# A dilated sliding attention with its feed-forward: ones written later and in blocks, one store on GpSimd, one q copy ahead of its reader

## The chip, the core and the metric

The kernel runs on one core of one Trainium2 chip. A core has four engines that compute, each with a queue of its own: TensorE (PE in the profile, its weight loads PEld), VectorE (DVE), ScalarE (ACT) and GpSimd (POOL). SyncE (SP) only issues transfers. Transfers run on 16 DMA engines and are issued from the queues of SP, ACT and POOL. The time of a run is device microseconds (us) from its begin to its end; lower is better. The change is judged by the median over runs.

## The reference

The inputs are q, k and v of shape 8 x 8 x 576 x 64 (batch, heads, tokens, width), and two weight matrices, w_in (512 x 2048) and w_out (2048 x 512). All are float32, and so is the output, of 4608 rows (8 x 576 tokens) by 512.

```python
rel = pos[:, None] - pos[None, :]
mask_plain = (rel >= 0) & (rel < window)                                    # window = 32
mask_dil = (rel >= 0) & (rel < window * dilation) & (rel % dilation == 0)   # dilation = 4
# heads 0..3 use mask_plain, heads 4..7 use mask_dil
scores = np.where(mask, scale * q @ k.T, -1e9)
attn = softmax(scores)
x = (attn @ v).transpose(0, 2, 1, 3).reshape(4608, 512)
h = np.maximum(x @ w_in, 0.0)
out = h * h @ w_out
```

## The kernel before, in words

Everything is computed in bfloat16 with float32 sums. The kernel is one long list of steps recorded in a fixed order; there is no loop on the chip. Each engine executes its own part of that list in order, and waits on semaphores where an operand or a buffer comes from another engine or from a transfer. Transfers have semaphores of their own, DMAHW0 to 7 for SP and ACT and DMASW0 to 7 for POOL, taken in turn; an issue first waits for the transfer that had its semaphore before it.

The feed-forward goes over tiles of tokens: four of 256 at first (two halves of each of two tiles), then seven of 512, 4608 tokens in all. Its work is cut into numbered groups. After each group some attention work for a later tile is recorded. Which work stands after which group is written out by hand in tables of strings: PROGRAM for batches 0 to 2 and the loads, STEPS for parts of batches 2 to 4 (an entry "57 2E20 ..." means: after group 57), STEADY for the tiles from token 1536 on, ALONE and LAST for the last two.

Attention works per batch on pairs of heads e = 0 to 3; e = 2 and 3 hold the dilated heads. Tokens are kept by their residue mod 4. For batches from 3 on, q and k are transposed by the DMA (line L334, issued by SP), and small vector copies then put border pieces where both halves of the partitions can read them: code Q (L571) copies the last or the first 16 tokens of each residue of q, code R (L596) those of k. `quadrants` (its matmuls are L724) computes the scores of one pair of heads and, in the same visit, the value products of other pairs, as 64 x 64 matmuls. In STEPS, "3V032/22,23" after group 59 is such a visit: scores of batch 3's pair 2, products of batch 2's pairs 2 and 3. "3Q0" is the q copy of batch 3 for the lower 64 partitions, whose target columns the last matmuls of that visit read. "W1" to "W4" are sums of weight blocks (L1010, `cross_w`), used from the tile at token 1536 on. L757 and L759 scale the value products into xT, the input of the feed-forward; L1067 is the first feed-forward product of the tiles up to 1535, L1230 the second one of the first four, L1138 and L1318 the products of later tiles.

The softmax's row sums are matmuls whose weights are `ones`, 128 columns at the end part of the constant tile mk: a 64 x 64 block of ones on the two diagonal places, zeros elsewhere. They are first used at L925. `bias` is another part of mk, made on VectorE from mask patterns that are loaded into mk at the start (L1411, on ACT's queue); L849 puts it into the scores of batch 0. `idle` is an area of zeros on which TensorE runs warm-up matmuls (L792) at the start.

The kernel begins with these constants, while POOL issues the loads of q, k, v and the weights one after the other (L267, L294, L1464). `load_qk` makes one issue for q and one for k.

Results leave through `store` (L968): 128 rows of the output tile osb are cut where the residue or the batch changes, and each piece is one issue. A batch has 576 tokens, 144 for each residue, so a piece can be short. Except for some stores of the last tile, all of them are issued by SP, as soon as VectorE (L1326) or ScalarE (L1347) has written the rows.

Of the kernel before, what the change touches and what calls it, by code (L numbers as in the profile page):

```python
# [75 lines left out]
FORKED = "BCD", "MNAB"  # L76
STEPS = (
# [33 lines left out]
def kernel(  # L111
# [9 lines left out]
    nc = tc.nc  # L121
    P = nc.NUM_PARTITIONS
    B, H, S, D = q.shape
# [43 lines left out]
    ones = mk[:, 256 + P : 256 + 2 * P]  # L167
# [613 lines left out]
    sides = [slice(64 * hl, 64 * hl + 64) for hl in range(2)]  # L781
# [172 lines left out]
    def store(osb, pos: int, c0: int = 0, c1: int = DM, engines=(nc.sync,)):  # L954

        x = turns = 0
        while x < P:
            b, y = divmod(pos + x, S)
            part = int(y >= RES * MN[0]) if b in PARTED else 0
            w = MN[part] if b in PARTED else M  # L960
            r, m = divmod(y - RES * MS[part], w)
            n, first = min(P - x, w - m), RES * (MS[part] + m) + r
            if b == B - 1:
                r, m = divmod(y, 16) if y < 64 else divmod(y - 64, 128)
                n, first = (16, RES * m + r) if y < 64 else (min(P - x, 128 - m), 64 + RES * m + r)
            row = b * S + first
            engine = engines[turns % len(engines)]
            engine.dma_start(out[row : row + RES * (n - 1) + 1 : RES, c0:c1], osb[x : x + n, c0:c1])  # L968
            x += n
            turns += 1  # L970
# [50 lines left out]
    def ffn_groups(tk0: int, nt: int):  # L1021
# [200 lines left out]
        def g2(m, part):  # L1222
            if part == 0:
                cur[m] = ps_f.tile([P, DM], f32, name="pf")
            x = m % 2 if per == 1 else m
            for f in range(4 * part, 4 * part + 4):
                n = 1 + ((tk0, m, part) in HALVED)
                for y in range(n):
                    cs = slice(y * DM // n, (y + 1) * DM // n)
                    nc.tensor.matmul(  # L1230
                        cur[m][:, cs],
                        h2[:, m // 2 if per == 1 else hh, HF * (f % 2) + f // 2, P * x : P * x + P],
                        w_out_sb[:, f, cs],
                        start=(f == 0 and y == 0), stop=(f == NF - 1), skip_group_check=True,
                    )
            if part == 3:
                slot = slots[0] = (slots[0] + 1) % (NT // P)
                nc.scalar.copy(osb[:, slot, :], cur[m][:, :])
                store(osb[:, slot, :], tk0 + (P * m + half) % nt if over else tk0 + P * m)
# [14 lines left out]
        def g2_small(code):  # L1254
# [8 lines left out]
            if code[0] == "P":  # L1263
                nm, a, b, fresh = {
                    "P1": ("y", b11, b_of[:, 0, 0], True), "P2": ("x", b12, b_of[:, 1, 0], True),
                    "P3": ("z", b12, b_of[:, 1, 1], False), "P4": ("y", b22, twin[1], False),
                    "P5": ("z", b21, t1, True), "P6": ("y", sm, t2, False), "P7": ("y", b11, twin[0], False),
                }[code[:2]]
                for k in range(*{"a": (0, HF // 2), "b": (HF // 2, HF), "": (0, HF)}[code[2:]]):
                    nc.tensor.matmul(  # L1270
                        place(nm), a[:, k, :], b[:, k, :], start=fresh and k == 0, stop=(k == HF - 1),
                        skip_group_check=True,
                    )
            elif code in "suz":
                to, nm = {"s": (outs[1][0], "y"), "u": (outs[0][1], "y"), "z": (outs[1][1], "z")}[code]
                nc.scalar.copy(to, place(nm))
            elif code in "ABCD":
                to, a, b, op = {"A": (b21, b21, b22, ALU.add), "B": (sm, b21, b11, ALU.subtract),
                                "C": (b11, b22, sm, ALU.subtract), "D": (b12, b12, sm, ALU.subtract)}[code]
                nc.vector.tensor_tensor(out=to, in0=a, in1=b, op=op)  # L1280
            elif code == "21":
                nc.scalar.copy(outs[1][0], place("y"))
                store(osb[:, cur["slots"][1], :], tk0 + P)
            else:
                to, nm = {"11": (outs[0][0], "x"), "12": (outs[0][1], "z"), "22": (outs[1][1], "y")}[code]
                nc.vector.tensor_tensor(out=to, in0=place(nm), in1=outs[1][0] if code == "11" else to, op=ALU.add)
                if code == "12":
                    store(osb[:, cur["slots"][0], :], tk0)
# [126 lines left out]
        nc.vector.memset(t[64:128, :, :, 0:64], 0.0)  # L1415

    nc.vector.memset(idle[:, :], 0.0)
    nc.vector.memset(ones[:, :], 0.0)
    for rows in sides:
        nc.vector.memset(ones[rows, rows], 1.0)  # L1420
    plain = osb[:, 0, :].rearrange("p (e i d) -> p e i d", e=2, d=D)
    for e in range(2):
        for hl, rows in enumerate(sides):
# [3 lines left out]
    for es, bs in ((slice(0, NE // 2), slice(0, NB)), (slice(NE // 2, NE), slice(8, NB))):  # L1427
        for hl in range(2):
            to = vbd[0][64 * hl : 64 * hl + 64, es, bs, 64 - 64 * hl : 128 - 64 * hl]
            none = idle[64 * hl : 64 * hl + 64, 0:64].unsqueeze(1).unsqueeze(1).broadcast_to(list(to.shape))  # L1430
            nc.scalar.copy(to, none)
    nc.vector.tensor_scalar(out=bias, in0=mk[:, 0:256], scalar1=-1.0, scalar2=30000.0, op0=ALU.add, op1=ALU.mult)
    far_end = osb[:, 1, 0:128].rearrange("p (e d) -> p e d", e=2)
    for hl, rows in enumerate(sides):
        nc.sync.dma_start(far_end[rows, :, :], v[0, H // 2 + hl : H : 2, 512:S, :].rearrange("h p d -> p h d"))
# [157 lines left out]
```

## Time and profile before

| what | value |
|---|---|
| median of 3 runs | 281.95 us (281.3 to 281.96) |
| the profiled execution | 281.38 us |
| its span, first to last instruction | 279.6 us |
| granted TensorE clock, mean | 0.997 |
| TensorE busy | 271.4 us, 97% of the span |
| VectorE, ScalarE, GpSimd busy | 227.6, 206.2 and 128.5 us |
| moved by DMA | 36.93 MB |

A row of the timeline or of the chain begins with its start and its duration in us, then the engine, the line of the kernel, the operation with what it writes and reads, the number of instructions merged into the row, and in brackets the idle time of the engine before it and what ended that. SPq, ACTq and POOLq are the queues that issue transfers. Rows of grouped lines end with busy us and the mean ns of one. A row on DMA issues ends with the time from issue to landing in us. A tile's number is left out in names: qk holds the transposed q and k, qb and kb what was loaded of them, pt the weights of the softmax, rec the reciprocals of its sums, h2T the hidden layer; pf, pa, po and pd are PSUM tiles.

### The profile page before, as it was taken

To read this page: it belongs to the slowest core of one execution; us is meant where nothing else is said; L and a number is where in the kernel's file an instruction comes from. 1 tells how busy PE (TensorE), PEld (TensorE's weight loads), DVE (VectorE), ACT (ScalarE), POOL (GpSimd) and SP (SyncE) were. 2 spreads that over 40 slices of the span, in tenths; PEclk is the share of its full clock that TensorE was granted. 3 is DMA by queue.
4 is the path that set the end of the run, shared out by engine and by line. 5 is a ranking of instruction groups with operands and counts; after the bars stand their busy time and mean duration, and the time that the engine had idled before them with its cause. 6 is when DMAs were issued, how large, how long until landed. Compare 5 with 4: busy or idle time off the path is not lost.

```text
span 279.6 us, 9042 instructions
## 1 busy us (share of the span) xinstructions
PE 271.4 (97%) x3681; PEld 234.4 (84%) x3687; DVE 227.6 (81%) x475; ACT 206.2 (74%) x457; POOL 128.5 (46%) x209
## 2 busy tenths in 40 slices
PE   7899999999999999999999999999999999999994
PEld 3679988997954578899889988988898899989983
DVE  0886998787789987879977997899699778965973
ACT  6888768887986878898689778977886667327620
POOL 8769973484872687764784359750000000000000
PEclk9999999999999999999999999999999999999998
DMA  8999999999999999999989996930310040013003
GB/s 127 198 193 213 207 152 220 196 144 212 187 193 225 153 172 198 183 198 173 166 83 221 193 149 94 181 26 4 98 55 2 2 152 0 2 38 113 4 24 129
DMA packets 83786, 36.93 MB, mean 132 GB/s; under 512 B 52736, under 2 KB 78464, under 8 KB 83744
## 3 DMA queue, kind: packets, MB, share of 16 engines
q0 software_dynamic: 49040, 18.53, 58.1%
q1 hardware_dynamic: 33728, 17.33, 30.9%
q10 hardware_dynamic: 976, 0.49, 0.7%
q8 instruction: 29, 0.48, 0.7%
q14 instruction: 13, 0.11, 0.1%
HBM read 37.31 MB, written 9.44 MB: 167 GB/s over the span
## 4 chain that ended last, share of the span: by engine, by line
PE 93%; DMA 2%; issue 1%; ACT 1%; DVE 1%; POOL 0%; POOLq 0%
PE pf L1318 31%; PE pf L1067 15%; PE pf L1138 10%; PE pf L1230 7%; PE pa L1138 7%; PE pd L1138 5%; PE po L1138 4%; PE pf L1270 2%; DMA kb<-in_k_dram 2%; PE pa L724 2%; PE pf L724 1%; PE po L724 1%; PE pa L354 1%; PE pd L724 1%; PE pa L819 1%
## 5 line engine op out<-in xcount | busy, mean ns | idle before, releaser
L1318 PEld LDWEIGHTS <-h2T 128*128 128x128 bf16 x680 | 64.4, 98 | 9.0 <-DVE h2T L1349 0.2
L1318 PE MATMUL pf<-w_out_sb,h2T 128*128 128x256 bf16 x448 | 53.4, 273 | 0.0
L552 POOL DMA_DIRECT2D vbd<-in_v_dram x80 | 42.9, 545 | 19.8 <-DMA vbd<-in_v_dram 5.8
L1067 PE MATMUL pf<-xT,w_in 128*128 128x256 bf16 (+1 forms) x319 | 44.6, 294 | 0.7 <-issue 0.7
L968 POOL DMA_DIRECT2D out_dram<-osb x1 | 0.6, 610 | 88.3 <-DVE osb L1326 88.3
L1067 PEld LDWEIGHTS <-w_in 128*128 128x128 bf16 x320 | 34.3, 114 | 7.9 <-issue 1.4
L1138 PEld LDWEIGHTS <-w_in 128*128 128x128 bf16 x288 | 31.6, 114 | 0.9 <-issue 0.3
L1080 ACT ACTIVATE h2T<-pf 128x512 bf16<-128x512 f32 x48 | 26.6, 603 | 4.8 <-PE pf L1067 4.5
L1347 ACT COPY osb<-pf 128x512 f32<-128x512 f32 x22 | 12.8, 583 | 19.3 <-PE pf L1318 16.4
L1200 DVE TENSOR_TENSOR h2T<-h2T 128x1024 bf16<-128x1024 bf16 x40 | 26.1, 683 | 0.1
L1230 PE MATMUL pf<-w_out_sb,h2T 128*128 128x256 bf16 (+1 forms) x139 | 22.5, 305 | 0.5 <-issue 0.3
L1326 DVE TENSOR_TENSOR osb<-pf,osb 128x512 f32<-128x512 f32 (+1 forms) x22 | 14.8, 674 | 7.8 <-ACT rec L741 5.1
L1138 PEld LDWEIGHTS <-qb 128*128 128x128 bf16 x192 | 21.0, 113 | 0.0
L1146 ACT ACTIVATE h2T<-pf 128x512 bf16<-128x512 f32 x28 | 16.8, 619 | 1.7 <-PE pf L1138 1.7
L1230 PEld LDWEIGHTS <-h2T 128*128 128x128 bf16 x144 | 13.2, 98 | 5.1
L544 POOL DMA_DIRECT2D vbd<-in_v_dram x20 | 12.1, 620 | 10.4 <-DMA qb<-in_q_dram 4.6
L1138 PE MATMUL pf<-xT,w_in 128*128 128x256 bf16 x112 | 16.8, 273 | 0.0
L1150 DVE CUSTOM_DVE_ANT_0 h2T<-pf,kb 128x512 bf16<-128x512 f32 x16 | 10.6, 685 | 7.3 <-PE pf L1138 5.2
L288 POOL DMA_DIRECT2D vbd<-in_v_dram x16 | 10.9, 689 | 10.9 <-DMA kb<-in_k_dram 4.9
L538 POOL DMA_DIRECT2D vd<-in_v_dram x20 | 12.2, 624 | 5.5 <-DMA kb<-in_k_dram 3.4
L750 ACT ACTIVATE rec<-rec 128x576 f32<-128x576 f32 x22 | 14.2, 688 | 0.3
L1085 DVE TENSOR_TENSOR h2T<-h2T 128x1024 bf16<-128x1024 bf16 (+1 forms) x20 | 11.4, 583 | 3.3 <-ACT h2T L1080 2.9
(267 smaller groups left out, 697.3 us busy)
## 6 DMA issues: line engine op xcount, KB each, us to landing
out_dram<-osb SPq DMA_DIRECT2D x20, 128.0 KB, 5.3
qb<-in_q_dram POOLq DMA_DIRECT2D x7, 320.0 KB, 8.6
kb<-in_k_dram POOLq DMA_DIRECT2D x7, 320.0 KB, 11.1
vd<-in_v_dram POOLq DMA_DIRECT2D x32, 64.0 KB, 6.7
w_in<-in_moe_w_in_dram POOLq DMA_DIRECT2D x4, 512.0 KB, 7.5
w_out_sb<-in_moe_w_out_dram POOLq DMA_DIRECT2D x4, 512.0 KB, 11.8
qb<-in_q_dram POOLq DMA_DIRECT2D x7, 256.0 KB, 7.5
kb<-in_k_dram POOLq DMA_DIRECT2D x7, 256.0 KB, 9.8
```

Of the source, the lines that this page charges most:

```text
L552: nc.gpsimd.dma_start(v_rows[b % 2][p0 + 16 * r : p0 + 16 * r + 16, e, :, :], v[b, 2 * e + hl, :, :].rearrange("(i m r) d -> r m i d", r=R ...
L724: nc.tensor.matmul(out, lhs, rhs, start=begin, stop=True, skip_group_check=True)
L750: nc.scalar.activation(rec[:, :], rec[:, :], ACT.Exp, scale=-1.0)
L1067: nc.tensor.matmul(to, w_in_sb[piece][:, kt, c0 : c0 + 509 : 4], rhs, start=(kt == kts[0] and x == 0), stop=(kt == kts[-1] and x == per - ...
L1080: nc.scalar.activation(hv, acc[u][:, :].rearrange("p (x n) -> p x n", x=2), ACT.Relu)
L1138: nc.tensor.matmul(home(nm)[:, g, :], wk[:, c0 + g : c0 + g + 127 * step + 1 : step], rhs[:, kt, :], start=fresh and kt == 0 and g == 0, s ...
L1146: nc.scalar.activation(to, home(nm), ACT.Relu)
L1200: nc.vector.tensor_tensor(out=part, in0=part, in1=part, op=ALU.mult)
L1230: nc.tensor.matmul(cur[m][:, cs], h2[:, m // 2 if per == 1 else hh, HF * (f % 2) + f // 2, P * x : P * x + P], w_out_sb[:, f, cs], start=( ...
L1318: nc.tensor.matmul(bank(nm, m, cs.start)[:, m, cs], a[:, k, P * m : P * m + P], w[:, cs], start=fresh and k == ks[0] and (m == 0 or nm == ...
L1326: nc.vector.tensor_tensor(out=to[:, at, cs], in0=src[:, at, cs], in1=other[:, at, cs], op=ALU.add)
L1347: nc.scalar.copy(bank("x") if code == "s" and forked_out else to, bank(nm))
```

## The change

It has three parts.

1. The zeroing of `ones` moves behind the bias. The two blocks of ones, 64 x 64 each, are then written by sixteen memsets of 64 x 8 in place of two.
2. In `store`, a piece of exactly 16 rows of batch 6 (B - 2) is issued by GpSimd in place of SP. There is one such piece in the program.
3. In STEPS, the copy 3Q0 stands after group 57 in place of group 60.

```diff
-    "3R01 | 58 W1 | 59 W2 3V032/22,23 2L2 W4 | 60 3Q0 W3 2X2 2L3 | 61 2X3 | 62 3Y0 | 63 3E20 | 64 3Y1 3K0 | 65 "
+    "3R01 3Q0 | 58 W1 | 59 W2 3V032/22,23 2L2 W4 | 60 W3 2X2 2L3 | 61 2X3 | 62 3Y0 | 63 3E20 | 64 3Y1 3K0 | 65 "
...
-            engine = engines[turns % len(engines)]
+            engine = nc.gpsimd if b == B - 2 and n == 16 else engines[turns % len(engines)]
...
     nc.vector.memset(idle[:, :], 0.0)
-    nc.vector.memset(ones[:, :], 0.0)
-    for rows in sides:
-        nc.vector.memset(ones[rows, rows], 1.0)
...
     nc.vector.tensor_scalar(out=bias, in0=mk[:, 0:256], scalar1=-1.0, scalar2=30000.0, op0=ALU.add, op1=ALU.mult)
+    nc.vector.memset(ones[:, :], 0.0)
+    for hl, rows in enumerate(sides):
+        for x in range(64 * hl, 64 * hl + 64, 8):
+            nc.vector.memset(ones[rows, x : x + 8], 1.0)
```

On VectorE, at the begin of the program, with the semaphores that each row waits for (DMAHW2 is the load of the mask patterns, Activation is ScalarE):

```order
 L1417 MEMSET qk 128x128
-L1418 MEMSET mk 128x64
-L1420 MEMSET mk 64x64 [waits DVE_49]
-L1420 MEMSET mk 64x64
-L1432 TENSOR_SCALAR mk<-mk 128x256 [waits DMAHW2_49]
+L1429 TENSOR_SCALAR mk<-mk 128x256 [waits DMAHW2_49]
+L1430 MEMSET mk 128x64
+L1433 MEMSET mk 64x8 [waits DVE_49]
+L1433 MEMSET mk 64x8 x15
 L834 COPY qk<-pa 128x256 [waits Activation_49] x2
```

The bias (TENSOR_SCALAR) now follows the zeroing of `idle` directly, and all memsets of `ones` stand between it and the first copy of transposed data.

On VectorE, around the visit after group 59 (L571 is 3Q0, the L596 copies are 3R00 and 3R01, the L1010 rows W1, W2, W4 and W3; DMAHW2 is here the transposed q):

```order
 L596 COPY qk<-qk 64x128 [waits DMAHW1_49]
 L596 COPY qk<-qk 64x128
+L571 COPY qk<-qk 64x4x2x16 [waits DMAHW2_49]
 L1010 TENSOR_TENSOR qb_96<-w_in_88 128x1024 [waits DMASW2_49,DMASW0_49,Pool_49]
 L1010 TENSOR_TENSOR qb_96<-qb_96,w_in_87 128x1024 [waits DMASW0_49,DVE_49]
 L1010 TENSOR_TENSOR qb_96<-w_in_87,qb_96 128x1024 [waits DMASW4_49,DVE_49]
-L571 COPY qk<-qk 64x4x2x16 [waits DMAHW2_49,PE_49]
 L1010 TENSOR_TENSOR qb_96<-w_in_87,w_in_88 128x1024 [waits DMASW1_49]
-L757 TENSOR_TENSOR xT<-po,rec 128x4x128 [waits Activation_49]
+L757 TENSOR_TENSOR xT<-po,rec 128x4x128 [waits PE_49,Activation_49]
```

The copy moved ahead of three sums. Its wait for TensorE is gone (before, it waited for the matmuls of the visit that read its target), and L757 now carries the wait for TensorE. On TensorE, in that visit, the 18th of the 20 score matmuls and its neighbours:

```order
 L724 MATMUL pa<-qk 64x80
 L724 LDWEIGHTS qk [waits DVE_49]
-L724 MATMUL pa<-qk 64x64
+L724 MATMUL pa<-qk 64x64 [waits DVE_49]
 L724 LDWEIGHTS qk
 L724 MATMUL pa<-qk 64x64
```

The order of TensorE's instructions is the same; the first matmul that reads the copied columns now waits for VectorE. In the queue of POOL, at its end, one row is new:

```order
 L552 DMA vbd_104<-in_v_dram 16x9x64 [waits DMASW4_49]
 L552 DMA vbd_104<-in_v_dram 16x9x64 [waits DMASW5_49]
-L968 DMA out_dram<-osb 128x256 [waits DMASW6_49,DVE_49]
-L1588 UNCONDITIONAL_BRANCH
-L1588 ISA [waits barrier_Pool_Activation_PE_DVE_SP_gather]
+L968 DMA out_dram<-osb 16x512 [waits DMASW6_49,DVE_49,Activation_49]
+L968 DMA out_dram<-osb 128x256 [waits DMASW7_49,DVE_49]
+L1589 UNCONDITIONAL_BRANCH
+L1589 ISA [waits barrier_Pool_Activation_PE_DVE_SP_gather]
```

The store of 16 rows stands between POOL's last load and its one store of the last tile.

## The prediction

> **What bounds the kernel now.** I read the page's busy times first, then its chain, then busy time by stretches of the span, then the timeline at the three places that the change touches.
>
> ```profile
> PE 271.4 (97%) x3681; PEld 234.4 (84%) x3687; DVE 227.6 (81%) x475; ACT 206.2 (74%) x457; POOL 128.5 (46%) x209
> PE 93%; DMA 2%; issue 1%; ACT 1%; DVE 1%; POOL 0%; POOLq 0%
> 2.00:12.00 10.00, 8.74 (x173) 5.30 (x173) 3.97 (x11) 7.23 (x19) 9.59 (x16) 1.00 1.24 185
> 12.00:30.00 18.00, 17.34 (x267) 15.94 (x261) 13.65 (x31) 15.18 (x32) 14.50 (x16) 1.00 1.28 204
> 80.00:90.00 10.00, 9.83 (x125) 5.12 (x125) 9.31 (x22) 6.62 (x15) 3.41 (x7) 1.00 1.40 210
> 120.00:249.00 129.00, 129.00 (x1806) 117.37 (x1805) 112.86 (x201) 96.47 (x207) 43.55 (x78) 1.00 0.63 95
> 249.00:256.00 7.00, 6.99 (x65) 6.67 (x63) 2.40 (x4) 4.44 (x9) 0.00 (x0) 1.00 0.50 150
> ```
>
> The last five rows give, after the stretch and its length, the busy time of PE, PEld, DVE, ACT and POOL. TensorE is the chain (93%), and from 120 to 249 us it has no hole at all. An edit elsewhere can win only what TensorE idles in the edit's own stretch: 1.26 us at 2 to 12, 0.66 at 12 to 30, 0.17 at 80 to 90, 0.01 at 249 to 256. It can lose more, by making TensorE wait.
>
> **Part 1, the ones.** Before, VectorE writes them in three memsets and then idles until the constants land; the bias follows, and then it idles again:
>
> ```profile
> 0.98 0.11 DVE L1418 MEMSET mk<- 128x64 uint32 x1
> 1.16 0.28 DVE L1420 MEMSET mk<- 64x64 bf16 x2
> 2.71 0.23 DVE L1432 TENSOR_SCALAR mk<-mk 128x256 bf16<-128x256 bf16 x1 [1.27 <-DMA mk<-mask_patterns]
> L1420 DVE MEMSET mk<- 64x64 bf16 x2 | 0.2, 112 | 0.1
> 6.62 0.38 ACT qk L833
> 7.03 0.76 DVE L834 COPY qk<-pa 128x256 bf16<-128x256 bf16 x2 [4.09 <-ACT qk L833]
> 10.05 0.21 PEld L925 LDWEIGHTS <-mk 128*128 128x128 bf16 x4
> ```
>
> The bias starts when its data lands (2.71 us) whether or not memsets stand ahead, so nothing is won there. Behind it now stand 17 memsets. A memset of a 64x8 block is not in the trace; the nearest row is 64x64 at 112 ns, and two of those took 0.28 us from start to end, so they start 0.28 - 0.112 = 0.168 us apart. From below: 17 x 0.112 = 1.9 us, done at 2.94 + 1.9 = 4.8. From above: 16 x 0.168 + 0.112, and some 0.06 for the wait on the zeroing (0.98 + 0.112 to 1.16): 2.9 us, done at 5.8. VectorE's next copy cannot start before ScalarE's copy ends (6.62 + 0.38 = 7.00), and TensorE's first weights from the ones load at 10.05. I take the upper end, since a row of several memsets shows that spacing: 1.2 us of cover stay. Without the cover (over 0.24 us per memset) each further 0.1 us would go straight into the copy at 7.03, which the chain passes through. Cost on the path: 0.
>
> The other neighbour is POOL, which issues the first loads through exactly this time:
>
> ```profile
> 1.27 0.74 POOL L267 DMA_DIRECT2D qb<-in_q_dram  x1 [0.82 <-POOLq L1577]
> 3.21 0.64 POOL L267 DMA_DIRECT2D kb<-in_k_dram  x1
> 6.29 0.84 POOL L1464 DMA_DIRECT2D w_in<-in_moe_w_in_dram  x1
> 7.78 0.64 POOL L267 DMA_DIRECT2D kb<-in_k_dram  x1
> 7.83 0.48 DVE L1414 MEMSET vbd<- 64x512 uint32 x1
> w_in<-in_moe_w_in_dram POOLq DMA_DIRECT2D x1, 512.0 KB, 6.7
> 13.57 0.45 PEld L1067 LDWEIGHTS <-w_in 128*128 128x128 bf16 x4 [0.22 <-issue]
> ```
>
> An issue of the same kind took 0.64 us beside an idle VectorE (3.21) and 0.64 us beside a VectorE memset (7.78 against 7.83), so I take no interference. The bounds: at most POOL slips by the whole memset time at 112 ns, 1.9 us; of that the first weights' load hides 13.57 - (6.29 + 6.7) = 0.58 us, leaving 1.3 us on TensorE. On the gain side, the first issue (0.74) ran beside the old memsets and would take 0.64 without them: 0.1 us off the first load, on which the chain starts. Taken: 0; ends -0.1 and +1.3.
>
> The Trainium skill, "SBUF — State Buffer", section "Who interferes with whom", says that a VectorE instruction with at most one SBUF input and outside the two-port modes does not contend with GpSimd; a memset has none, so by that rule the sum here is 0. The same page warns in its "DVE blocks DMA" box that VectorE copies from SBUF to SBUF can keep GpSimd from writing descriptors; if that held for memsets too, the sum would be the +1.3 us. The 7.78 row agrees with the first.
>
> **Part 2, the store.** One issue of 16 rows leaves SP's queue and joins POOL's.
>
> ```profile
> 248.00 1.51 DVE L1326 TENSOR_TENSOR osb<-pf,osb 128x512 f32<-128x512 f32 x2 [0.34 <-PE pf L1318]
> 249.54 0.33 SPq L968 DMA_DIRECT2D out_dram<-osb  x1
> 253.87 0.88 SPq L968 DMA_DIRECT2D out_dram<-osb  x2
> 266.67 0.59 ACT L1347 COPY osb<-pf 128x512 f32<-128x512 f32 x1 [1.15 <-PE pf L1318]
> 273.91 0.61 POOL L968 DMA_DIRECT2D out_dram<-osb  x1 [88.35 <-DVE osb L1326]
> 275.51 0.29 DVE osb L1326
> ```
>
> It is the first of the eleven that SP issues from 249.54 to 254.75 us, so the ten behind it go 0.33 us sooner. On POOL it costs what POOL's one store costs, 0.61 us, and it waits for the same VectorE sum (249.51). POOL has nothing else between 185 and 273.91 us, so nothing is queued behind it but the last quarter, 24 us later. The next writer of its output slot is the last tile's copy at 266.67 or later, some 14 us behind, so a store slower by any factor seen here is still hidden. SP's completion semaphores shift by one place; each stands for a store eight issues back, landed long before. The chain ends in the last VectorE sum (275.51 + 0.29 = 275.80) and its store, which keep their engines. Sum: 0; from the rows not below -0.01 (TensorE's whole idle there), not above +0.05.
>
> **Part 3, the q copy.** Now it stands ahead of three of the four weight sums of L1010, and the matmul that reads its columns waits for it.
>
> ```profile
> 73.70 1.48 SPq L334 DMA_TRANSPOSE qk<-qb  x1
> qk<-qb SPq DMA_TRANSPOSE x1, 6.4
> 81.56 0.52 DVE L596 COPY qk<-qk 64x128 bf16<-64x128 bf16 x2
> 82.10 0.69 DVE L1010 TENSOR_TENSOR qb<-w_in 128x1024 bf16<-128x1024 bf16 x1
> 83.55 0.69 DVE L1010 TENSOR_TENSOR qb<-w_in,qb 128x1024 bf16<-128x1024 bf16 x1
> 84.28 0.19 DVE L571 COPY qk<-qk 64x128 bf16<-64x128 bf16 x1
> 84.50 0.69 DVE L1010 TENSOR_TENSOR qb<-w_in,w_in 128x1024 bf16<-128x1024 bf16 x1
> 85.11 0.68 DVE L757 TENSOR_TENSOR xT<-po,rec 128x512 bf16<-128x512 f32 x1
> 86.44 0.68 DVE L757 TENSOR_TENSOR xT<-pf,rec 128x512 bf16<-128x512 f32 x1
> 82.55 0.20 PE pa L724 x20
> 87.17 0.01 issue
> 117.48 0.59 PE pd L1138 x4
> 87.18 2.92 PEld L1067 LDWEIGHTS <-w_in 128*128 128x128 bf16 x14 [0.27 <-issue]
> ```
>
> The copy's one remaining wait is for the transposed q, which landed at 73.70 + 6.4 = 80.1 us, 2 us ahead. So it follows the two L596 copies, from 82.1 to 82.3. Its reader is the 18th of the 20 matmuls that run from 82.55 to 82.75 on the chain, so at 82.7: 0.4 us to spare. The three sums behind it start about 0.2 us later; they feed the products of L1138, which first run at 117.48 us. The fourth sum needs no result of the third, so the gap where the copy stood closes: 84.50 - 84.24 = 0.26 us come back against 0.19 paid, and the L757 sums start where they did or up to 0.1 us sooner. TensorE's hole at 87.17, just behind the second L757 (ends 87.12), is 0.01 us on the chain and 0.27 us in weight loads. Taken: 0. From below -0.17 us (all of TensorE's idle at 80 to 90); from above +0.2 us (the copy's length, if every VectorE step slips by it into 87.17).
>
> **Sum.** 0 + 0 + 0. The profiled run took 281.38 us for a span of 279.6, 0.57 below the median of 281.95; the runs reach from 281.3 to 281.96, so the profile is of a run at their lower end. On the median I forecast 281.9 us. Differences under 0.3% (0.85 us) cannot be told from none here, since three runs of one kernel already spread by 0.66 us.
>
> **Rivals.** First, slower: the memsets hold up POOL's issues. For it speaks only that both run at 3 to 6 us; against it the equal issues of 0.64 us. Its full price is +1.3 us, 283.2 us, and it passes 0.3% once POOL slips by 0.85 + 0.58 = 1.43 us, that is 84 ns for each of 17 memsets. Chance 0.10. Second, slower by little: VectorE's line slips by the copy, or TensorE waits for it; +0.2 us, 282.1 us, for it the meeting at 87.12 and 87.17, against it the gap that closes. Chance 0.12, within 0.3% by itself. Third, faster: the first load goes 0.1 us sooner, and TensorE's 0.17 us of idle at 80 to 90 go: 281.6 us, or some 281.1 where the median also falls among the lower runs (281.3). For it the 0.74 beside the 0.64; against it that TensorE's idle at 2 to 30 has other causes. Chance 0.18, of which 0.10 pass 0.3% if something unseen adds to it. My forecast, no effect, has 0.55; 0.05 stay for a slowing that none of these names.
>
> So slower by over 0.3% gets 0.10 + 0.05 = 0.15, faster 0.10, the rest 0.75. The range runs from 281.0 (the third rival at the lowest run) to 282.9 (most of the first rival on the median), leaving 2 in 10 outside.
>
> **What would show it.** Right: the memsets end before 6 us, the copy of L834 still starts near 7.0; POOL's third to sixth issues still take 0.63 to 0.69 us and TensorE's first w_in weights load near 13.6; L571 runs near 82.1 and the 82.55 group has no hole; SP's ten stores end near 254.4; the chain still ends in the sums of 275 us. Wrong: an issue of POOL at 3 to 6 us over 0.75 us, VectorE still in memsets at 7 us, a TensorE wait on L571, or a new wait of VectorE or ScalarE for the POOL store at 266 to 273 us.

## The result: faster by 0.4%, and most of it not where the change was costed

The changed kernel takes 280.41 us, the median of 6 runs (279.94 to 280.76). The kernel before, timed beside it, takes 281.47 us (6 runs, 281.3 to 281.96). The ratio is 0.9958, with a 95% interval of 0.9948 to 0.9968. The forecast was 281.9 us and no effect. Of the 1.49 us between it and the measurement, 0.43 lie in the kernel before: the forecast stood on a median of 281.95 us of three runs, and six give 281.47. The change itself is the other 1.06. The profiled execution after took 280.44 us with a span of 278.7 us; before, the span was 279.6 us.

The page of the changed kernel, busy times and chain:

```profile
PE 271.4 (97%) x3687; PEld 234.2 (84%) x3687; DVE 228.3 (82%) x489; ACT 206.3 (74%) x457; POOL 129.0 (46%) x210
PE 94%; DMA 2%; ACT 1%; issue 1%; DVE 1%; POOL 0%; POOLq 0%
```

TensorE still is the chain and as busy as before. VectorE has 489 instructions in place of 475: the 14 more memsets. At the two places where the prediction had costed work, the timeline of the changed kernel shows this (VectorE, then POOL, at 2.5 to 8 us; VectorE at 81 to 87 us):

```profile
2.69 0.23 DVE L1429 TENSOR_SCALAR mk<-mk 128x256 bf16<-128x256 bf16 x1 [1.68 <-DMA mk<-mask_patterns]
3.05 0.39 DVE L1433 MEMSET mk<- 64x8 bf16 x16
7.00 0.76 DVE L834 COPY qk<-pa 128x256 bf16<-128x256 bf16 x2 [3.56 <-ACT qk L833]
3.22 0.65 POOL L267 DMA_DIRECT2D kb<-in_k_dram  x1
...
81.39 0.49 DVE L596 COPY qk<-qk 64x128 bf16<-64x128 bf16 x2
81.78 0.19 DVE L571 COPY qk<-qk 64x128 bf16<-64x128 bf16 x1
84.07 0.68 DVE L1010 TENSOR_TENSOR qb<-w_in,w_in 128x1024 bf16<-128x1024 bf16 x1
84.67 0.68 DVE L757 TENSOR_TENSOR xT<-po,rec 128x512 bf16<-128x512 f32 x1
86.00 0.68 DVE L757 TENSOR_TENSOR xT<-pf,rec 128x512 bf16<-128x512 f32 x1
```

The sixteen memsets are done at 3.44 us, POOL's issue beside them takes 0.65 us, and the copy of L834 starts at 7.00. The q copy stands ahead of the sums, and the gap that it left has closed: the first L757 sum starts 0.44 us sooner.

The end of the kernel differs. First VectorE's last sum, then the last store (issued by ScalarE's queue; the last number is us from issue to landing), then SyncE's waits at the end of the program (total, times, longest), before:

```profile
275.51 0.29 DVE L1326 TENSOR_TENSOR osb<-pd,osb 128x128 f32<-128x128 f32 x1
out_dram<-osb ACTq DMA_DIRECT2D x1, 128.0 KB, 2.4
SPq L1588 <- DMA out_dram<-osb: 2.8, 2, 2.0
L1588 SPq DRAIN  x3: 7/7/13, 278.8 to 279.1; - x3
```

and the same views after:

```profile
275.48 0.29 DVE L1326 TENSOR_TENSOR osb<-pd,osb 128x128 f32<-128x128 f32 x1 [0.15 <-PE pd L1318]
out_dram<-osb ACTq DMA_DIRECT2D x1, 128.0 KB, 1.9
SPq L1589 <- DMA out_dram<-osb: 1.9, 4, 0.7
L1589 SPq DRAIN  x3: 7/7/13, 277.8 to 278.1; - x3
```

The last sum ends at 275.80 us before and 275.77 after: up to there these two executions come out equal (what lies behind that is told with the copy below). From its end to the end of the span it takes 3.80 us before and 2.90 after. I call this stretch the tail. Its two parts, in the records of the trace:

- The last store lands 2.36 us after its issue before, and 1.89 after.
- From that landing to the end of the span it takes 1.36 us before, and 0.92 after.

Together 0.03 + 0.47 + 0.44 us, which is the whole difference of the spans. The busy time of the engines shows nothing of it, since no engine computes there.

**The first part is an instruction fetch.** DMA by queue kind, and the busy tenths of the DMA engines in 40 slices, first from 276 to 277 us and then from 277 to 278, before:

```profile
q10 hardware_dynamic: 183, 0.17, 50.1%
q1 hardware_dynamic: 153, 0.13, 40.8%
q14 instruction: 1, 0.01, 1.9%
...
DMA  9996682200010010101011010110101000000000
```

The same stretch, 277 to 278 us, after (from 276 to 277 us its list holds only q10 and q1):

```profile
DMA  7956542100000000000000000000000000000000
```

q14 carries instructions in packets of 8192 bytes, and not VectorE's alone. It has thirteen of them in the span, before and after. Eight lie within 0.9 us of each other in the two executions. The other five move with the 14 instructions that VectorE has more: from 37.25, 80.21, 137.78, 196.59 and 276.48 us to 26.89, 76.55, 131.33, 190.12 and 263.49. I take these five for VectorE's. Before, the last one starts at 276.48 us, 0.97 us behind the start of the last sum, and holds one of the 16 DMA engines for 309 ns. The last store is spread over all 16. Fifteen have finished their share 1.89 us after the issue; the one with the packet takes until 2.36. That is the row of single ones from 277.2 to 277.8 us. After, it lies at 263.49 us and the slices are empty from 277.2 us.

**The second part is the order in which SyncE waits.** At the end of the program SyncE waits for the transfers' semaphores in nine waits, one after the other and always in the same order; for one that is already done the next wait starts 0.062 us later. Before, the last store had the second semaphore of that list, and seven waits followed once it had landed: 7 x 0.062 = 0.43 us. In the view of waits SyncE waits twice, 2.0 us of it at once. After, one store fewer from SyncE shifts the semaphores by one place, and the last store has the last one on the list: four short waits while the stores land one by one, and nothing behind the last.

### The profile page after: what moved, and what is told of

Same layout as the page of the kernel before. It is cut to its first block, busy times and chain, and to the rows that moved or that the text cites. A ratio compares the mean times of both kernels' runs of the same rounds, so it can differ in the third digit from the quotient of the medians.

```text
span 278.7 us, 9063 instructions
## 1 busy us (share of the span) xinstructions
PE 271.4 (97%) x3687; PEld 234.2 (84%) x3687; DVE 228.3 (82%) x489; ACT 206.3 (74%) x457; POOL 129.0 (46%) x210
## 4 chain that ended last, share of the span: by engine, by line
PE 94%; DMA 2%; ACT 1%; issue 1%; DVE 1%; POOL 0%; POOLq 0%
PE pf L1318 31%; PE pf L1067 15%; PE pf L1138 11%; PE pf L1230 8%; PE pa L1138 7%; PE pd L1138 5%; PE po L1138 4%; PE pf L1270 2%; PE pa L724 2%; DMA kb<-in_k_dram 2%; PE pf L724 1%; PE po L724 1%; PE pa L354 1%; PE pd L724 1%; PE pa L819 1%
## 5 line engine op out<-in xcount | busy, mean ns | idle before, releaser
L1230 PE MATMUL pf<-w_out_sb,h2T 128*128 128x256 bf16 (+1 forms) x144 | 23.3, 308 | 0.0
L267 POOL DMA_DIRECT2D qb<-in_q_dram x18 | 13.2, 735 | 3.4 <-DMA vbd<-in_v_dram 1.8
```

The source lines that it names most:

```text
L267: nc.gpsimd.dma_start(t[0:n, part, hs, :], src[b, hs, t0 : t0 + RES * n, :].rearrange("h (p r) d -> p h (r d)", r=RES))
L1230: nc.tensor.matmul(cur[m][:, cs], h2[:, m // 2 if per == 1 else hh, HF * (f % 2) + f // 2, P * x : P * x + P], w_out_sb[:, f, cs], start=( ...
```

## The experiments

The working theory was these two parts, with the first owed to the number of VectorE's instructions (part 1 of the change adds 14) and the second to part 2. The rival was that one of the parts wins its time in the body, where the prediction had looked for it. In the table, "added" is the number of VectorE instructions added ahead of 30 us. "Gap" is the time between VectorE's wait ahead of a sum of L981 (at 35 us; used further below) and that sum. "Fetch" is the start of the last q14 packet against the start of the last sum. "Landed" is from the issue of the last store to its landing, "behind" from there to the end of the span, and "tail" is the stretch defined above. All these come from the one profiled execution. "Median" is less the median of the kernel before in the same job. All in us. The ratios in the text, with their 95% intervals, are not taken from these medians and can differ from them: the 0.9977 of e8 is 0.65 us, its median 1.00.

| kernel | added | gap | fetch | landed | behind | tail | median |
|---|---|---|---|---|---|---|---|
| before | 0 | 0.47 | +0.97 | 2.36 | 1.36 | 3.80 | |
| after | 14 | 0.07 | -11.99 | 1.89 | 0.92 | 2.90 | -1.06 |
| e1 ones only | 14 | 0.07 | -12.16 | 1.97 | 1.35 | 3.41 | -0.81 |
| e2 store only | 0 | 0.48 | +1.00 | 2.39 | 0.92 | 3.40 | -0.46 |
| e3 copy only | 0 | 0.48 | +0.98 | 2.37 | 1.35 | 3.81 | -0.08 |
| e4 two memsets | 0 | 0.47 | +1.00 | 2.38 | 0.92 | 3.39 | -0.59 |
| e5 memsets ahead | 14 | 0.07 | -12.15 | 1.89 | 0.92 | 2.90 | -1.27 |
| e6 four memsets | 2 | 0.07 | -1.49 | 1.90 | 0.92 | 2.92 | -1.21 |
| e7 eight memsets | 6 | 0.06 | -5.85 | 1.89 | 0.92 | 2.90 | -1.25 |
| e8 four stores | 14 | 0.06 | -11.88 | 1.93 | 1.11 | 3.13 | -1.00 |
| e9 four, old place | 2 | 0.06 | -1.30 | 1.90 | 1.35 | 3.34 | -0.87 |
| e10 one column each | 128 | 0.43 | +1.02 | 2.41 | 0.92 | 3.42 | -0.63 |
| e11 without the copy | 14 | 0.07 | -12.14 | 1.89 | 0.92 | 2.90 | -1.00 |
| e12 changed, again | 14 | 0.07 | -12.16 | 1.90 | 0.92 | 2.91 | -1.34 |
| e13 pad at 49 us | 0 | 0.48 | -1.56 | 2.14 | 1.35 | 3.58 | -0.14 |
| e14 pad at 110 us | 0 | 0.48 | -1.56 | 2.16 | 1.36 | 3.60 | -0.04 |
| e15 pad at 249 us | 0 | 0.48 | -1.56 | 2.14 | 1.35 | 3.58 | -0.22 |

### Each part alone

Part 1 on the kernel before (e1):

```diff
-    nc.vector.memset(ones[:, :], 0.0)
-    for rows in sides:
-        nc.vector.memset(ones[rows, rows], 1.0)
...
+    nc.vector.memset(ones[:, :], 0.0)
+    for hl, rows in enumerate(sides):
+        for x in range(64 * hl, 64 * hl + 64, 8):
+            nc.vector.memset(ones[rows, x : x + 8], 1.0)
```

> Part 1 alone. Fetch theory: 14 more VectorE instructions move the last 8192-byte instruction packet out of the final stores, the last store lands some 1.9 us after its issue instead of 2.4, and the time falls by 0.45 us (ratio 0.9984), with SyncE still walking through its other final waits after that store. Rival (all of the gain comes from the store's move): 0. Rival (the start became faster): TensorE's first matmul on loaded data before 6.2 us, and the body shorter by 0.5 us or more.

Part 2 on the kernel before (e2):

```diff
-            engine = engines[turns % len(engines)]
+            engine = nc.gpsimd if b == B - 2 and n == 16 else engines[turns % len(engines)]
```

> Part 2 alone. Wait-order theory: the last store gets the semaphore that SyncE waits for last (before: the second in its list), so the seven or so waits of 0.06 us each no longer follow it: 0.43 us less (ratio 0.9985), while the instruction packet stays at 276 to 277 us and the last store still lands 2.4 us after its issue. Rival (all of the gain comes from the memsets): 0. Rival (the shorter SP queue): a shorter body, TensorE's last matmul earlier.

Part 3 on the kernel before (e3):

```diff
-    "3R01 | 58 W1 | 59 W2 3V032/22,23 2L2 W4 | 60 3Q0 W3 2X2 2L3 | 61 2X3 | 62 3Y0 | 63 3E20 | 64 3Y1 3K0 | 65 "
+    "3R01 3Q0 | 58 W1 | 59 W2 3V032/22,23 2L2 W4 | 60 W3 2X2 2L3 | 61 2X3 | 62 3Y0 | 63 3E20 | 64 3Y1 3K0 | 65 "
```

> Part 3 alone. Both tail theories: 0 within 0.1 us, TensorE's last matmul at the same time within 0.1 us, the copy near 82.1 us. Rival (the copy frees VectorE's line ahead of TensorE): 0.2 us less, with no hole of TensorE left at 80 to 90 us.

And the changed kernel with two memsets in place of sixteen, so that parts 2 and 3 and the place behind the bias stay, but no instruction is added (e4):

```diff
-        for x in range(64 * hl, 64 * hl + 64, 8):
-            nc.vector.memset(ones[rows, x : x + 8], 1.0)
+        for x in range(64 * hl, 64 * hl + 64, 64):
+            nc.vector.memset(ones[rows, x : x + 64], 1.0)
```

> The changed kernel with two memsets of ones behind the bias instead of sixteen, so that only the number of VectorE's instructions goes back. Fetch theory: the instruction packet is back at 276 to 277 us and the time is 0.43 us below the kernel before (ratio 0.9985), half of the whole change. Rival (the place of the ones, behind the bias, is what counts): the full gain of 1.1 us stays (0.9958).

Against a common 281.66 us the medians are 280.85 (ratio 0.997, interval 0.9952 to 0.9988), 281.2 (0.9989, 0.9966 to 1.0013), 281.58 (0.9989, 0.9969 to 1.0009) and 281.07 (0.9967, 0.9943 to 0.999). Timed alone, then, part 2 and part 3 cannot be told from no change. The tails can: in their profiles the first two take out one of the two pieces each, and only that one. With the ones alone the last fetch lies at 264.26 us and the store lands after 1.97 us, but the wait order stays (1.35 behind). With the store alone the order changes (0.92 behind), and the fetch is where it was, and the landing takes 2.39. With two memsets, the fetch is back at +1.00 although the other edits are there. The copy alone leaves the tail as it was.

### What counts about the ones: their place, their size or their number

The sixteen memsets ahead of the bias (e5; the opposite move of the edit), four and eight memsets behind it (e6, e7; 32 and 16 columns each, shown for four), and the kernel before with nothing changed but four memsets for two, in the old place (e9):

```diff
# e5
     nc.vector.memset(idle[:, :], 0.0)
+    nc.vector.memset(ones[:, :], 0.0)
+    for hl, rows in enumerate(sides):
+        for x in range(64 * hl, 64 * hl + 64, 8):
+            nc.vector.memset(ones[rows, x : x + 8], 1.0)
...
-    nc.vector.memset(ones[:, :], 0.0)
-    for hl, rows in enumerate(sides):
-        for x in range(64 * hl, 64 * hl + 64, 8):
-            nc.vector.memset(ones[rows, x : x + 8], 1.0)
# e6 (e7: 16 for 32)
-        for x in range(64 * hl, 64 * hl + 64, 8):
-            nc.vector.memset(ones[rows, x : x + 8], 1.0)
+        for x in range(64 * hl, 64 * hl + 64, 32):
+            nc.vector.memset(ones[rows, x : x + 32], 1.0)
# e9, on the kernel before
-    for rows in sides:
-        nc.vector.memset(ones[rows, rows], 1.0)
+    for hl, rows in enumerate(sides):
+        for x in range(64 * hl, 64 * hl + 64, 32):
+            nc.vector.memset(ones[rows, x : x + 32], 1.0)
```

> The changed kernel with its sixteen memsets ahead of the bias again. Fetch theory: the number of VectorE's instructions counts and not their place, so the full gain stays, ratio to the kernel before 0.9958 within 0.0010. Rival (the place behind the bias wins): about half of the gain is lost, 0.998 or above.

> The changed kernel with four memsets of ones (64x32): two VectorE instructions more than before instead of 14. Fetch theory: the packet comes two instructions sooner, near 275.5 us, still among the last stores; the last store lands late by 0.3 to 0.5 us, ratio to the kernel before 0.998 to 0.9985. Rival (each further instruction helps in proportion): one seventh of part 1's gain.

> The changed kernel with eight memsets of ones (64x16): six VectorE instructions more than before. Fetch theory: the packet comes at 271 to 274 us, ahead of the last three stores, and the full gain is there already: ratio 0.9958 to 0.9965. Rival (in proportion): 3/7 of part 1's gain, 0.998.

> The kernel before with four memsets of ones (64x32) instead of two, still ahead of the bias, and nothing else: two more VectorE instructions. Fetch theory: the last instruction packet comes near 274 us instead of 276.5 and the last store lands 1.9 to 2.0 us after its issue; from the last VectorE sum to the end 3.4 us instead of 3.8, the time 0.4 us less (ratio 0.9986). Rival (the number of instructions also speeds the body, as the 0.8 us of part 1 alone could mean): 0.7 us less or more.

The ratios are 0.9961 (0.993 to 0.9992), 0.9959 (0.9935 to 0.9983), 0.9951 (0.9933 to 0.9968) and 0.996 (0.9941 to 0.9979). The place does not matter. Nor do sixteen: two more instructions on VectorE already move the fetch from 0.97 us behind the start of the last sum to 1.3 or 1.5 ahead of it. For four memsets I had expected the fetch at about 275.5 us and a loss. That missed: it came at 273.96, VectorE's last instructions being spread over more time than I had reckoned, and the gain was there in full.

If it is the number that counts, a whole block more of instructions should bring the loss back. A packet of 8192 bytes is a block of 128 if an instruction takes 64 bytes. In e10 the ones of the changed kernel are written a column at a time, and the zeroing in three pieces: 128 instructions more than before.

```diff
-    nc.vector.memset(ones[:, :], 0.0)
+    for x0, x1 in ((0, 48), (48, 96), (96, 128)):
+        nc.vector.memset(ones[:, x0:x1], 0.0)
     for hl, rows in enumerate(sides):
-        for x in range(64 * hl, 64 * hl + 64, 8):
-            nc.vector.memset(ones[rows, x : x + 8], 1.0)
+        for x in range(64 * hl, 64 * hl + 64):
+            nc.vector.memset(ones[rows, x : x + 1], 1.0)
```

> The changed kernel with the ones written by 128 memsets of one column and the zeroing cut in three: 128 VectorE instructions more than the kernel before. Fetch theory: an 8192-byte packet holds 128 instructions of 64 bytes, so the packets fall where they fell before, one again at 276 to 277 us; the last store lands 2.4 us after its issue, 3.4 us from the last VectorE sum to the end, ratio to the kernel before 0.9983 and not 0.9958. Rival (more instructions, or more memset time at the start, help): 0.9958 or below. If the memsets ran past 7 us, the first copies would start late and show it there.

The fetch is back at 276.26 us, +1.02, and the store lands after 2.41 us. DMA by queue kind in e10, from 276 to 277 us:

```profile
q14 instruction: 1, 0.01, 1.9%
```

The median is 281.04 us (ratio 0.9972, 0.9956 to 0.9988), as in e4, which adds no instruction. So the period is 128, and the position of the code in its blocks is the cause.

The Trainium skill, "Runtime: NRT & Kernel Launch", section "Instruction fetch mechanics", says that instructions are refilled in blocks of 16 KiB (256 instructions), and that crossing into a new one costs one bump of a DMA tail and is mostly hidden. The 29 packets of another instruction queue here, q8, do have 16384 bytes (29 x 256 = 7424, near the 3687 matmuls and 3687 weight loads of TensorE), but VectorE's have 8192. In the tail the fetch is not hidden from the last store: 0.47 us. The measurement decides.

### The order of the waits

In e8, four pieces of batch 6 go to GpSimd in place of one. Three stores fewer from SyncE shift the semaphores by three places more; three waits then follow the one of the last store.

```diff
-            engine = nc.gpsimd if b == B - 2 and n == 16 else engines[turns % len(engines)]
+            engine = nc.gpsimd if b == B - 2 and n in (16, 112, 32, 96) else engines[turns % len(engines)]
```

> The changed kernel with four stores of batch 6 on GpSimd instead of one: the first four pieces of that tile. Wait-order theory: the last store gets the semaphore three places ahead of the last in SyncE's final list, three waits of 0.06 us follow it, so 0.19 us are given back: ratio 0.9964 to 0.9968. Rival (fewer issues on SyncE are what helps): faster than the changed kernel, below 0.9955.

Of the 0.44 us, 0.19 are given back (1.11 us behind the landing for 0.92, which is 3 x 0.062), and nothing else in the tail moved by more than 0.04 us. The median is 280.62; the ratio, 0.9977 (0.9953 to 1.0), lies above the 0.9964 to 0.9968 that I had expected. SyncE's waits of e8:

```profile
SPq L1589 <- DMA out_dram<-osb: 2.0, 3, 1.2
```

So the store's gain does not come from a lighter queue: with three issues fewer on SP the tail is longer by 0.23 us, and the median lies 0.2 to 0.3 us above those of e5 to e7 in the same job, though the intervals of their ratios overlap. Which semaphore the last store happens to have decides.

### The copy

The changed kernel without part 3 (e11: the table line as before), and the changed kernel once more beside it (e12, no edit):

```diff
-    "3R01 3Q0 | 58 W1 | 59 W2 3V032/22,23 2L2 W4 | 60 W3 2X2 2L3 | 61 2X3 | 62 3Y0 | 63 3E20 | 64 3Y1 3K0 | 65 "
+    "3R01 | 58 W1 | 59 W2 3V032/22,23 2L2 W4 | 60 3Q0 W3 2X2 2L3 | 61 2X3 | 62 3Y0 | 63 3E20 | 64 3Y1 3K0 | 65 "
```

> Parts 1 and 2 without part 3. Theory: TensorE's hole at 80 to 90 us is back, 0.17 us more than the changed kernel, 2.9 us from the last VectorE sum to the end. Rival (the copy's place is without effect): the same time as the changed kernel, and the stretch from 81.8 to 90.6 us as short as there.

> The changed kernel itself, beside the other three. Theory: 0.4 + 0.4 + 0.17 us, about 1.0 us less than the kernel before (ratio 0.9965), 2.9 us from the last VectorE sum to the end. Rival (a further 0.3 us in the body from the memsets): 0.9955 or below.

The medians are 280.67 (0.9974, 0.9945 to 1.0003) and 280.33 (0.9943, 0.9923 to 0.9963): 0.34 us apart, with intervals that overlap. The profiles are sharper. From one and the same weight load of TensorE at 81.8 us to another at 90.6 us it takes 8.78 us in e11, and 8.75 to 8.84 in the kernel before, e1, e2 and e9, none of which has the copy moved. In all kernels with the copy moved it takes 8.62. In the kernel before the whole difference is one step, at the place that the prediction had named: the load at 87.18 us comes 0.39 us behind the one ahead of it, where the step is 0.22 in the changed kernel. Busy time in the stretch from 80 to 90 us (columns as in the prediction), after:

```profile
80.00:90.00 10.00, 10.00 (x127) 5.22 (x125) 9.48 (x23) 6.79 (x16) 3.23 (x6) 1.00 1.44 222
```

TensorE has no hole left there, where it had 0.17 us. This row alone would not show it, since e9, with the copy in its old place, has 10.00 too; the loads do. So part 3 wins 0.13 to 0.22 us.

Against the kernel before, TensorE's weight loads start 0.17 us sooner at 82 us and 0.34 us sooner from 91 to 127 us, in the profile after and in that of e12 alike. (The first 0.17 come at 22 to 26 us, where the profile before has a wait of 0.13 us that comes and goes between kernels without a pattern.) In e12 the 0.34 stay to the last load, and the last sum ends at 275.47 us. In the profile after 0.31 of them are lost again: 0.20 at 137 us and the rest at 129 to 131 and 157 to 158. The list of waits from 125 to 160 us has these rows, and that of e12 has none like them:

```profile
PEld L1318 <- DVE h2T L1200: 0.3, 2, 0.2
PEld L1318 <- issue: 0.2, 1, 0.2
```

The two waits for VectorE stand at 131 and 158 us; the idle time at 137, where most was lost, ends in no wait that the profile shows. That is how the body could look untouched in the first comparison: what one execution lost there covered the gain. What made VectorE late, and TensorE idle at 137 us, in that execution is open.

### What was left over, and where it went

The pieces did not add up for kernels with VectorE instructions added at the start. For e1 the tail accounts for 0.39 us of 0.81, and for e9 for 0.46 of 0.87, while e2 and e3 fit within 0.1. Four memsets of an unused tile were therefore put on VectorE in the kernel before, aimed at 45, 105 and 250 us; they ran at 48.6, 109.7 and 249.3 (e13, e14 and e15; after group 30, 84 and 258):

```diff
+    spare = const.tile([P, 16], bf16, name="spare")
...
+        if g == 30:
+            for x in range(0, 8, 2):
+                nc.vector.memset(spare[:, x : x + 2], 0.0)
```

> The kernel before with four small memsets of an unused tile on VectorE at about 45 us, so that every later instruction of VectorE stands four places further on in its instruction blocks, and every earlier one where it stood. The fetch that lay at 276.5 us moves ahead of the last stores, the fetch at 37 us stays. Theory A (the 0.4 us of the tail are all that a shift of the fetches is worth, the rest of what the runs with a shift from the start showed is spread): the tail is 3.35 to 3.45 us, 0.4 below the kernel before, and the median of runs 0.4 below it, against 0.81 and 0.88 where the shift stood at the start. Theory B (the fetch at 37 us costs something in the body as well): also 0.4 here, since that fetch stays. Theory C (a later fetch, at 190 or 262 us, costs the body something): 0.8 here.

> As in the pad at 45 us, with the four memsets at about 105 us. Fetches up to there stay where they were, the later ones move. Theories A and B: median 0.4 us below the kernel before, tail 3.35 to 3.45. Theory C: 0.8.

> As in the pad at 45 us, with the four memsets at about 250 us, behind every fetch but the last two. Theories A and B: median 0.4 us below the kernel before, tail 3.35 to 3.45. Theory C: 0.4 as well, unless the fetch at 262 us is the one that costs. If this is 0.4 and the pad at 45 us 0.8, a fetch between them costs 0.4; if all three pads are 0.4, what the shifts from the start gave above it belongs to the first fetches (B) or to spread (A), which these runs then leave apart only by their intervals.

The ratios are 0.9984 (0.996 to 1.0009), 1.0 (0.9991 to 1.0008) and 1.0005 (0.9987 to 1.0022). All three theories had expected 0.4 us or more; by their medians the pads won 0.2 at most. (The ratio of e13 alone would still allow 0.4; those of e14 and e15 allow 0.25 and 0.37 at most.) The traces say why, and bear on the remainder. The sums in the tail of e13, then POOL's last store:

```profile
270.65 0.68 DVE L1327 TENSOR_TENSOR osb<-pf,osb 128x512 f32<-128x512 f32 x1
273.53 1.83 DVE L1327 TENSOR_TENSOR osb<-pf,osb 128x512 f32<-128x512 f32 x3 [2.20 <-issue]
274.52 0.60 POOL L969 DMA_DIRECT2D out_dram<-osb  x1 [87.38 <-DVE osb L1327]
```

In the kernel before, the sum that starts at 273.53 here stands at 272.92:

```profile
272.92 1.51 DVE L1326 TENSOR_TENSOR osb<-pf,osb 128x512 f32<-128x512 f32 x2 [1.85 <-issue]
```

VectorE's wait ahead of it ends 2.63 us before the start of the last sum in both. The sum then starts 0.05 us later in the kernel before, and 0.40 us later in all three pads, and the fetch packet follows behind it. This 0.35 us makes the stores behind it late, POOL's and one of SyncE's by 0.35 us and the next two by 0.13, and the last store takes 2.14 us in place of 1.9. That these late stores hold it up on the DMA engines is my reading. So the pads moved the packet out of the last stores and put a stall of VectorE in its place. The tail's 0.2 us is what their medians show, within 0.16.

The same stall stands in the body, at the "gap" of the table. VectorE's timeline at 34 to 36 us, before:

```profile
34.26 0.69 DVE L1280 TENSOR_TENSOR s2T<-h2T 128x1024 bf16<-128x1024 bf16 x1
35.37 0.69 DVE L981 TENSOR_TENSOR w_diff<-w_out_sb 128x1024 bf16<-128x1024 bf16 x1 [0.42 <-issue]
```

after, where the sum starts as soon as its wait has ended:

```profile
34.09 0.69 DVE L1280 TENSOR_TENSOR s2T<-h2T 128x1024 bf16<-128x1024 bf16 x1
34.74 0.69 DVE L981 TENSOR_TENSOR w_diff<-w_out_sb 128x1024 bf16<-128x1024 bf16 x1
```

and in e10, with 128 instructions more, where it is back:

```profile
35.05 0.69 DVE L981 TENSOR_TENSOR w_diff<-w_out_sb 128x1024 bf16<-128x1024 bf16 x1 [0.39 <-issue]
```

The gap is 0.43 to 0.48 us in all eight kernels with no instruction added ahead of it, or exactly 128, and 0.06 to 0.07 in all nine with 2, 6 or 14. Counting VectorE's records in the traces places the stall exactly. The late sum at 35 us is the 64th record in the kernel before and in the other six with nothing added ahead of it, and the 192nd in e10. In e10 the 64th record is one of the memsets, and the same stall stands there, again with no wait in the profile:

```profile
4.51 2.06 DVE L1434 MEMSET mk<- 64x1 bf16 x72 [0.37 <-issue]
```

The late sum in the tail of the three pads is the 576th record. All these are 64 and a multiple of 128. Other records at such places start without a gap (the 320th and the 448th in e10), so not every one stalls. The copies L385 that VectorE makes behind the sum at 35 us are read by TensorE's weight loads of L1270 at 41 us. In the list of waits of e4, which has the stall, from 39 to 43 us:

```profile
PEld L1270 <- DVE qk L385: 0.5, 1, 0.5
```

The ten weight loads around that wait take 1.09 to 1.50 us, 1.31 on average, in the eight kernels with the stall. They take 1.10 to 1.19 us, 1.12 on average, in the nine without. So VectorE's 0.40 us cost TensorE 0.19 us on average, between 0 and 0.4 in single executions. The kernel before and e15 show none of it (1.10 and 1.09): in the kernel before, TensorE came to these loads 0.16 us later than in e4, and VectorE's copies L385 ran 0.25 us sooner.

With the tail, 0.15 us for the copy and this 0.19 us, the sum for the change is 0.90 + 0.15 + 0.19 = 1.24 us, against medians of 1.06 and 1.34 in two jobs; for e5, e6, e7 and e8 the sums are 1.24, 1.22, 1.24 and 1.01 against 1.27, 1.21, 1.25 and 1.00. For e1 and e9 0.23 us each stay unexplained, within what medians of 12 runs leave open. That the stall is the change of instruction block is my reading: its places 128 apart are shown, and so is a fetch packet behind each; what the engine does in those 0.40 us no record shows.

No version beat the changed kernel; the medians of e5, e6, e7 and e12 lie within 0.08 us of its 280.41.

## Why the prediction was wrong

**Part 1, the ones.** As to time the step held, with room to spare: sixteen memsets took 0.39 us, most of them starting 14 to 17 ns apart, not the 2.9 us of the upper end, POOL's issues beside them did not stretch, and L834 started at 7.00 us. What failed is what was counted. The step counted the time of 17 memsets and never their number as instructions. Fourteen more shift every later VectorE instruction against its fetch blocks. That is worth 0.47 us in the landing of the last store, and 0.19 us at TensorE's loads of L1270. "Cost on the path: 0" should have been a gain of 0.47 us, and of about 0.66 with the second, which only averages over the traces show.

**Part 2, the store.** POOL's issue held (it took 0.52 us for the 16 rows, and nothing waited for it). That "the ten behind it go 0.33 us sooner" did not: SyncE's last seven pieces wait for ScalarE's copy of their rows, which ends at 251.26 us, so the first of them starts at 251.28 us in place of 251.37 and the last ends at 254.71 in place of 254.75. That cost nothing. The failing sentence is "SP's completion semaphores shift by one place; each stands for a store eight issues back, landed long before". It looked at what waits when a semaphore is used again, and not at the end of the program, where SyncE waits for all of them in order. And "The chain ends in the last VectorE sum ... and its store, which keep their engines. Sum: 0" ended the path at a store, when 3.80 us of the span lie behind that sum. The bounds of -0.01 to +0.05 were drawn from TensorE's idle time, which says nothing of a stretch in which TensorE has finished. The term measured -0.44 us.

**Part 3, the q copy.** The mechanism was right, down to the 0.17 us that TensorE could win back. The size was off: taken 0, measured -0.13 to -0.22. The step had noted that the gap gives back 0.26 us against 0.19 paid, let the L757 sums come up to 0.1 us sooner, and put that to nothing. They came 0.44 us sooner, 0.27 of it beyond the 0.17 that TensorE was ahead by then, and TensorE's late load at 87.18 us was gone.

**The sum and the rivals.** "An edit elsewhere can win only what TensorE idles in the edit's own stretch" is the sentence on which all three bounds stood, and it is wrong twice. An added instruction acts far from its place, through the blocks of all the code behind it, and the last stretch of the span has idle time that belongs to no edit's stretch. The first rival (POOL held up) and the second (VectorE slips) did not happen. The third had the sign and TensorE's 0.17 us. It passed the 0.3% as it had foreseen, "if something unseen adds to it", but the first load did not go sooner (POOL's first issue still took 0.74 us). The result lies 0.6 us below the lower end of the range, which was set by TensorE's holes. Nearly every sign listed as "right" appeared (SyncE's ten stores, as said, did not end near 254.4; one of POOL's issues took 0.71 us, just above its bound of 0.69), and none listed as "wrong". The time was still off, because none of these signs was of what lies behind the last sum.

## What to carry to other kernels

Read the tail of the trace as a stage of its own: from the last computing instruction to the end of the span, ask which transfer lands last, what shares its DMA engines, and how many waits SyncE has left behind it. When an edit adds or removes instructions, look where that engine's fetch packets (q14 here for VectorE) fall before, and which come to lie among transfers or ahead of an instruction on the path: the count of instructions can be worth more than their time. Gains of this kind are a matter of position, and the next edit that adds an instruction or a store can take them away again.

## What the runs showed of the hardware that I had not expected

- VectorE's instructions come in packets of 8192 bytes, one for each 128 of them, over the DMA engines that carry the data. One packet of 309 ns among the last stores delayed one engine's share of the last store by 0.47 us.
- VectorE stalls about 0.4 us at certain instructions with no wait recorded. In the traces these are its 64th, 192nd or 576th record: the place moves with the number of instructions ahead, and comes back after 128.
- SyncE's waits at the end cost 0.062 us each, in a fixed order, also for transfers that landed long ago. The semaphore of the last store decides between 0.92 and 1.36 us.
- Sixteen memsets of 64x8 on VectorE start 14 to 17 ns apart, with one step of 106 ns between the two blocks, 0.39 us in all. Two of 64x64 took 0.28 us.
